# A fused linear attention and GELU network: four edits to the weight sums, the last loads and the last group of tokens

## The chip, the cores and the metric

The kernel runs on one core of one Trainium2 chip. The metric is the device time of one execution in microseconds (us), as the median of several runs. TensorE multiplies matrices into PSUM, VectorE and ScalarE read PSUM and work on SBUF, GpSimd works on SBUF, and SyncE and ScalarE issue the DMA transfers.

## The reference

Two stages follow each other. The first is linear attention over 8 batches, 8 heads, 576 tokens and a head size of 64; the second is a two-layer network on the 4608 tokens that come out.

```python
phi = lambda x: np.where(x > 0, x, np.exp(x) - 1.0) + 1.0
q_p, k_p = phi(q), phi(k)
kv = np.einsum('bhsd,bhse->bhde', k_p, v)
z = np.sum(k_p, axis=2)
attn = np.einsum('bhsd,bhde->bhse', q_p, kv) / (np.einsum('bhsd,bhd->bhs', q_p, z)[..., None] + 1e-06)
x = attn.transpose(0, 2, 1, 3).reshape(4608, 512)
h = x @ w_in                       # 512 -> 2048
g = 0.5 * h * (1 + tanh(c * (h + 0.044715 * h**3)))
out = g @ w_out                    # 2048 -> 512
```

## The kernel before

**Tiles and groups.** The tokens are worked in nine groups of 512. Groups 0 to 7 hold the first 512 tokens of one batch each (MAIN = 512). The last 64 tokens of each batch (REST = 64), 512 in all, make group 8, which the code calls j == B. In group 8, tile t of 128 tokens holds the rest of batches 2t and 2t + 1, one behind the other: partitions 0 to 63 are of the first batch and 64 to 127 of the second.

**One group.** `iteration(j)` runs steps in an order that is written out by hand, and after each step it runs whatever was registered for that slot with `at(j, slot, ...)`. Each engine takes its instructions in this program order, so a slot is also a place in every engine's queue. A group has 16 h steps: `h_mm` (line 390) multiplies a block of 128 columns of w_in with the transposed x into a PSUM bank of 512 columns, and `gelu` (line 400) writes the result to `g` in SBUF as f16. From group 2 on, the product g @ w_out is not formed directly. `Products` takes g and w_out as 2 x 2 blocks and forms seven block products (line 767) in place of eight, in the manner of Strassen and Winograd. This needs sums of blocks of w_out, formed once by `sum_w_out` (line 739), and sums of blocks of g, formed in each group by `Products.sums` and `last_sum` (line 750). The partial results p, z and w stay in PSUM and are added on VectorE by `plus` (line 820) or copied by ScalarE (lines 789 and 803) into two result tiles o1 and o2, which are stored.

**The attention for the next group** runs in between. For phi, ScalarE forms the exponential (`exp_of`, line 220), VectorE the linear part (`linear_of`, line 228) and the smaller of the two (`least_of`, line 234); `cast_v` (line 239) converts v. The products of k and v (line 250), the numerator and denominator (`nab_quads`, line 328) and the division (line 284) follow. Transposes go through the DMA on SyncE's queue (lines 645, 657 and 680).

**Sums of w_out.** `sum_w_out` is four subtractions of [128, 8, 256] in f16. They are given to GpSimd in halves, so eight instructions. The first three write `w_sum` and stand at slot 10 of group 1; the fourth overwrites a quarter of w_out itself and stands at slot 0 of group 2. The first use is in group 2.

**Rest tokens.** `load_rest(m)` fetches q of the rest of batches 2m and 2m + 1 (line 117, two transfers of 128 KB). m = 0 and 1 are loaded at slot 2 of group 4; m = 2 and 3 at slot 1 of group 6. `plan_rest(m)` puts their linear part at slot 6, their exponential at slot 15 and their minimum with its DMA transpose at slot 18, of group 5 for m = 0 and 1 and of group 6 for m = 2 and 3. The tiles that hold phi of the rest tokens come two at a time, so the second pair takes the place of the first.

**Group 8's end.** There is no next group behind which a store could hide. Step 5 stores o2 whole and step 6 first stores the low half of o1 (`self.store(0, self.o1, lo)`). Step 6 then forms the last product in two halves of 128 tokens, both into halves of one PSUM bank z, adds each half and stores it. `store_rest` (line 825) issues two transfers for a tile, one for each batch, on ScalarE's and SyncE's queues:

```python
for s, eng in enumerate((nc.scalar, nc.sync)):
    r0 = (2 * t + s) * S + MAIN
    eng.dma_start(out=out[r0 : r0 + REST, fs], in_=o_sb[REST * s : REST * (s + 1), fs])
```

PSUM has a pool of six banks for h, p, z, w and the like, and a pair of banks for the attention.

Of the kernel before, what the change touches and what calls it, by code (L numbers as in the profile page):

```python
# [10 lines left out]
FP16 = mybir.dt.float16  # L11
AF = mybir.ActivationFunctionType
ALU = mybir.AluOpType
# [3 lines left out]
def kernel(  # L17
# [16 lines left out]
    nc = tc.nc  # L34

    B, H, S, D = q.shape
    d_model, d_ff = moe_w_in.shape
    P = 128
    HP = P // 2
    C = 4  # L40
    MAIN = P * C
    REST = S - MAIN
# [3 lines left out]
    MM = d_ff // P  # L46
    E = D + 1
    N2 = d_model // 2
# [9 lines left out]
    pg = ctx.enter_context(tc.tile_pool(name="pg", bufs=1))  # L58
# [19 lines left out]
    def bank(name, shape, dt=FP32):  # L78
        return ps_b.tile(shape, dt, name=name, tag="b")
# [150 lines left out]
    def least_of(name, b, hs=None):  # L230
        p, e = phi[name, b], exps[name, b]
        if hs:
            p, e = p[:, :, hs, :], e[:, :, hs, :]
        nc.vector.tensor_tensor(p, p, e, op=ALU.min)  # L234
# [153 lines left out]
    def h_mm(h_ps, xt, m, ts=slice(0, MAIN), blocks=range(KM)):  # L388
        for c in blocks:
            nc.tensor.matmul(  # L390
                h_ps[:, ts],
                lhsT=w_in_sb[:, c, P * m : P * (m + 1)],
                rhs=xt[:, c, ts],
                start=(c == 0),
                stop=(c == KM - 1),
                skip_group_check=True,
            )

    def gelu(g, m, h_ps):
        nc.scalar.activation(  # L400
            g[:, :, m, :], h_ps.rearrange("p (a n) -> p a n", a=2), AF.Gelu_apprx_tanh
        )

    h_begun = {0: {}, 1: {}}

# [104 lines left out]
    def at(j, slot, fn, *args):  # L510


        fill.setdefault((j, slot), []).append((fn, args))
# [124 lines left out]
    def plan_rest(m):  # L638
        j = 5 + m // 2

        def least():
            least_of("qr", m)
            if m == 0:
                qts[B] = pt.tile([P, C, NP, P], BF16, name="qt")
            nc.sync.dma_start_transpose(
                out=qts[B][:, m], in_=phi["qr", m][:, 0].rearrange("p h d -> p (h d)")
            )

        at(j, 6, linear_of, "qr", m)
        at(j, 15, exp_of, "qr", m)  # L650
        at(j, 18, least)

# [63 lines left out]
    def o_mm(o_ps, g, t, ms, half=None):  # L716
        for m in ms:
            if m == ms.start + 2 and half:
                run(*half)
            nc.tensor.matmul(  # L720
                o_ps,
                lhsT=g[:, t // 2, m, P * (t % 2) : P * (t % 2 + 1)],
                rhs=w_out_sb[:, :, m, :],
                start=(m == 0),
                stop=(m == MM - 1),
            )
# [4 lines left out]
    def sum_w_out(ns):  # L731

        b11, b21 = (w_out_sb[:, 0, h] for h in ff)
        b12, b22 = (w_out_sb[:, 1, h] for h in ff)
        t1, t2, t4 = (w_sum[:, n] for n in range(3))
        sums = ((t1, b12, b11), (t2, b22, t1), (t4, b21, t2), (b12, b22, b12))
        for out, i0, i1 in sums[ns]:
            for ms in (slice(0, 4), slice(4, 8)):
                nc.gpsimd.tensor_tensor(out[:, ms], i0[:, ms], i1[:, ms], op=ALU.subtract)  # L739

    ff = (slice(0, MM // 2), slice(MM // 2, MM))

    class Products:
# [18 lines left out]
            self.subtract(self.a[0][0], self.a[0][1], self.s[1])  # L762

        def product(self, ps, lhs, rhs, first, ts=range(2)):
            for t in ts:
                for m in range(MM // 2):
                    nc.tensor.matmul(  # L767
                        ps[:, t, :],
                        lhsT=lhs[:, m, P * t : P * (t + 1)],
                        rhs=rhs[:, m, :],  # L770
                        start=(first and t == 0 and m == 0),
                        stop=(m == MM // 2 - 1),
                        skip_group_check=True,
                    )

        def step(self, n):
            j = self.j
            (a11, a12), (a21, a22) = self.a
            (b11, b21), (t3, b22) = [[w_out_sb[:, d, h] for h in ff] for d in range(2)]
            t1, t2, t4 = (w_sum[:, i] for i in range(3))  # L780
            lo, hi = slice(0, N2), slice(N2, d_model)
            if n < 4:
                ps = bank("o_ps", [P, 2, N2])
            if n == 0:
                self.p = ps
                self.product(ps, a11, b11, True)
                self.o1 = pout.tile([P, 2, d_model], FP32, name="o_sb")
                self.o2 = pout.tile([P, 2, d_model], FP32, name="o_sb")
                nc.scalar.copy(self.o1[:, :, hi], ps)
            elif n == 1:  # L790
                self.z = ps
                self.product(ps, self.s[0], t1, True)
            elif n == 2:
                self.product(ps, self.s[1], t2, True)
                self.plus(self.o1[:, :, hi], ps, self.o1[:, :, hi])
            elif n == 3:
                self.w = ps
                self.product(ps, a21, t3, True)
                self.plus(self.o2[:, :, hi], ps, self.o1[:, :, hi])
                self.plus(self.o2[:, :, hi], self.z, self.o2[:, :, hi])  # L800
            elif n == 4:
                self.product(self.p, a12, b21, False)
                nc.scalar.copy(self.o1[:, :, lo], self.p)  # L803
            elif n == 5:
                self.product(self.w, a22, t4, False)
                self.plus(self.o2[:, :, lo], self.w, self.o1[:, :, hi])
                self.store(1, self.o2)
            elif j < B:
                self.product(self.z, a11, b22, False)
                self.plus(self.o1[:, :, hi], self.z, self.o1[:, :, hi])  # L810
                at(j + 1, 0, self.store, 0, self.o1)
            else:
                self.store(0, self.o1, lo)
                for t in range(2):
                    self.product(self.z, a11, b22, False, (t,))
                    self.plus(self.o1[:, t, hi], self.z[:, t], self.o1[:, t, hi])
                    self.store_rest(t, self.o1[:, t], hi)

        def plus(self, out, i0, i1):
            nc.vector.tensor_tensor(out, i0, i1, op=ALU.add)  # L820

        def store_rest(self, t, o_sb, fs):
            for s, eng in enumerate((nc.scalar, nc.sync)):
                r0 = (2 * t + s) * S + MAIN
                eng.dma_start(
                    out=out[r0 : r0 + REST, fs], in_=o_sb[REST * s : REST * (s + 1), fs]
                )

        def store(self, h, o_sb, fs=slice(0, d_model)):

# [7 lines left out]

    def iteration(j):
        xt = xts[j]  # L840
        g = pg.tile([P, 2, MM, MAIN // 2], FP16, name="g")
        hs = [("h", m) for m in range(MM)]
        us = [range(m, m + 4) for m in range(0, MM, 4)]
        if j == 0:
            us[2:3] = range(8, 10), range(10, 12)
            steps = hs + [("o", t, u) for u in us for t in range(C)]
        elif j == 1:
            os = [[("o", t, u) for u in us[i : i + 2] for t in range(C)] for i in (0, 2)]
            steps = hs[:8] + os[0] + hs[8:] + os[1]
        else:  # L850
            products = Products(j, g)
            steps = [hs[i + n] for i in range(MM // 2) for n in (0, MM // 2)]
            steps += [("product", n) for n in range(7)]
            at(j, 7, products.sums, slice(0, 4))
            at(j, 15, products.sums, slice(4, 8))
            at(j, 16, products.last_sum)
        o_pss = {}
        for slot, step in enumerate(steps):
            if step[0] == "h":
                m = step[1]  # L860
                h_ps = h_begun.get(j, {}).get(m)
                if h_ps is None:
                    h_ps = bank("h_ps", [P, MAIN])
                    h_mm(h_ps, xt, m)
                gelu(g, m, h_ps)
            elif step[0] == "product":
                products.step(step[1])
            else:
                t, u = step[1:]
                if u.start == 0:  # L870
                    o_pss[t] = bank("o_ps", [P, d_model])
                o_mm(o_pss[t], g, t, u, half=(j, slot - 0.5))
                if u.stop == MM:
                    finish(j, t, o_pss[t])
            run(j, slot)
# [15 lines left out]
        at(b - 3, 1, load_all_pairs, "v", v, b)  # L891
    for m in range(2):
        at(4, 2, load_rest, m)
        at(6, 1, load_rest, m + 2)
    for j in range(2, 7):
        at(j, 16, gelu_table)
    at(1, 10, sum_w_out, slice(0, 3))
    at(2, 0, sum_w_out, slice(3, 4))

    for j in range(B + 1):  # L900
        iteration(j)
# [30 lines left out]
```

## Time and profile before

| what | value |
|---|---|
| time, median of 3 runs | 277.02 us (276.88 to 278.88) |
| span of the profiled execution | 274.5 us |
| TensorE busy, share of the span | 265.8 us, 97% |
| VectorE / ScalarE / GpSimd busy | 158.3 / 164.1 / 37.1 us |
| granted TensorE clock | 0.998 |
| HBM read and written | 36.70 and 9.44 MB, 168 GB/s over the span |

The span is what the profiler recorded of one execution. An engine's busy share is an average over all stages. In a line of the timeline the first number is the start in us from the span's start, the second the duration in us, then the engine, the line of the kernel, the operation, output<-input, the tile's form and the count; in brackets stands how long the engine had idled before, and which instruction ended that. Engines with a q behind them (SPq, ACTq) are the queues that issue DMA transfers.

### The profile page before, as it was taken

How to read it: one execution, taken by the hardware profiler on the slowest of the kernel's cores; microseconds unless marked ns; L12 is line 12 of the kernel's file. 1: busy time of each engine (PE TensorE's matmuls, PEld its weight loads, DVE VectorE, ACT ScalarE, POOL GpSimd, SP SyncE). 2: the span in 40 equal slices, each digit the busy share in tenths (PEclk: the TensorE clock that was granted, in tenths of full speed). 3: DMA queues.
4: the chain of work that ended last, by engine and by line, in shares of the span. 5: the costliest groups of instructions: out<-in, count | busy, mean ns of one | idle time of the engine just before them, and what ended most of it. 6: DMA issues, size and time to landing. Idle time of an engine off the chain costs nothing.

```text
span 274.5 us, 5840 instructions
## 1 busy us (share of the span) xinstructions
PE 265.8 (97%) x2485; PEld 165.9 (60%) x2485; DVE 158.3 (58%) x246; ACT 164.1 (60%) x224; POOL 37.1 (14%) x29
## 2 busy tenths in 40 slices
PE   8999999999999999999999999999989999999992
PEld 3584456444444686568656865686458646864781
DVE  3850286965669966788648874672376246422431
ACT  4768878794888683578357835763664365036400
POOL 3147309994000000000000000000000000000000
PEclk9999999999999999999999999999999999999999
DMA  7999999985999986993798650328521403030004
GB/s 245 401 406 398 409 405 403 401 326 154 162 331 276 397 123 187 331 264 73 185 389 222 84 189 2 79 47 153 146 57 41 171 2 76 2 153 0 2 0 153
DMA packets 59592, 53.84 MB, mean 196 GB/s; under 512 B 35760, under 2 KB 45488, under 8 KB 59568
## 3 DMA queue, kind: packets, MB, share of 16 engines
q1 hardware_dynamic: 56784, 44.58, 55.3%
q10 hardware_dynamic: 2784, 8.91, 9.0%
q8 instruction: 19, 0.31, 0.5%
q14 instruction: 5, 0.04, 0.0%
HBM read 36.70 MB, written 9.44 MB: 168 GB/s over the span
## 4 chain that ended last, share of the span: by engine, by line
PE 91%; DVE 3%; ACT 2%; DMA 1%; SPq 1%; issue 0%; DVEq 0%
PE h_ps L390 43%; PE o_ps L767 31%; PE o_ps L720 8%; PE w_ps L424 4%; DMA qr<-in_q_dram 1%; PE n_ps L328 1%; PE kv_ps L250 1%; PE n_ps L250 1%; DVE k_p L234 1%; PE n_ps L266 1%; ACT k_e L220 1%; PE t_ps L383 1%; ACT q_e L220 1%; SPq L117 1%; DVE s L750 0%; ACT L220 0%
## 5 line engine op out<-in xcount | busy, mean ns | idle before, releaser
L390 PE MATMUL h_ps<-xt,w_in_sb 128*128 128x512 bf16 (+1 forms) x628 | 128.9, 361 | 0.9 <-DVE xs L284 0.9
L400 ACT ACTIVATE g<-h_ps 128x512 f16<-128x512 f32 x144 | 84.6, 599 | 66.1 <-PE h_ps L390 65.4
L390 PEld LDWEIGHTS <-w_in_sb 128*128 128x128 bf16 x628 | 57.9, 98 | 63.4 <-DVE xs L284 1.3
L767 PEld LDWEIGHTS <-g 128*128 128x128 f16 x560 | 54.8, 98 | 8.5 <-issue 0.7
L767 PE MATMUL o_ps<-w_out_sb,g 128*128 128x256 f16 x448 | 52.5, 273 | 0.5 <-DVE o_sb L820 0.5
L820 DVE TENSOR_TENSOR o_sb<-o_ps,o_sb 128x512 f32<-128x512 f32 (+1 forms) x36 | 24.4, 677 | 30.2 <-PE o_ps L767 28.1
L750 DVE TENSOR_TENSOR s<-g 128x1024 f16<-128x1024 f16 x14 | 9.7, 690 | 36.5 <-ACT g L400 36.5
L720 PE MATMUL o_ps<-w_out_sb,g 128*128 128x512 f16 x128 | 29.4, 379 | 0.0
L284 DVE TENSOR_TENSOR xs<-n_ps,r 128x384 bf16<-128x384 f32 (+2 forms) x43 | 25.4, 592 | 1.5
L767 PE MATMUL o_ps<-w_sum,s 128*128 128x256 f16 x224 | 25.6, 273 | 0.0
L767 PEld LDWEIGHTS <-s 128*128 128x128 f16 x224 | 21.9, 98 | 2.5
L720 PEld LDWEIGHTS <-g 128*128 128x128 f16 x128 | 12.1, 98 | 13.3
L228 DVE TENSOR_SCALAR q_p<-q_x 128x2048 bf16<-128x2048 f32 (+1 forms) x9 | 10.5, 1171 | 13.1 <-DMA q_x<-in_q_dram 13.1
L220 ACT ACTIVATE k_e<-k_x 128x2304 bf16<-128x2304 f32 (+1 forms) x9 | 17.2, 1908 | 0.8 <-DMA k_x<-in_k_dram 0.8
L803 ACT COPY o_sb<-o_ps 128x512 f32<-128x512 f32 x7 | 4.1, 586 | 22.2 <-PE o_ps L767 22.2
L220 ACT ACTIVATE q_e<-q_x 128x2048 bf16<-128x2048 f32 (+1 forms) x9 | 15.5, 1719 | 2.8 <-DMA q_x<-in_q_dram 2.7
L228 DVE TENSOR_SCALAR k_p<-k_x 128x2304 bf16<-128x2304 f32 (+1 forms) x9 | 12.9, 1432 | 4.1 <-DMA k_x<-in_k_dram 4.1
L767 PE MATMUL o_ps<-w_sum,g 128*128 128x256 f16 x112 | 13.4, 273 | 0.0
L239 DVE CAST vp<-v_x 128x2304 bf16<-128x2304 f32 (+1 forms) x9 | 12.9, 1439 | 0.5 <-DMA v_x<-in_v_dram 0.4
L234 DVE TENSOR_TENSOR k_p<-k_p,k_e 128x2304 bf16<-128x2304 bf16 (+1 forms) x9 | 12.0, 1337 | 1.3 <-ACT k_e L220 1.0
L415 ACT ACT_TABLE_LOAD x9 | 11.5, 1283 | 0.2
L739 POOL TENSOR_TENSOR w_sum<-w_out_sb,w_sum 128x1024 f16<-128x1024 f16 x4 | 11.6, 2924 | 0.0
(61 smaller groups left out, 169.7 us busy)
## 6 DMA issues: line engine op xcount, KB each, us to landing
out_dram<-o_sb ACTq DMA_DIRECT2D x16, 512.0 KB, 4.9
k_x<-in_k_dram SPq DMA_DIRECT2D x7, 1152.0 KB, 7.0
v_x<-in_v_dram SPq DMA_DIRECT2D x7, 1152.0 KB, 12.2
q_x<-in_q_dram SPq DMA_DIRECT2D x6, 1024.0 KB, 12.5
w_st<-in_moe_w_in_dram SPq DMA_DIRECT2D x3, 1024.0 KB, 13.5
q_x<-in_q_dram SPq DMA_DIRECT2D x4, 512.0 KB, 8.6
w_st<-in_moe_w_out_dram SPq DMA_DIRECT2D x2, 1024.0 KB, 12.5
w_st<-in_moe_w_out_dram SPq DMA_DIRECT2D x4, 512.0 KB, 11.2
```

The lines of the kernel that those rows point to most:

```text
L220: nc.scalar.activation(o, i, AF.Exp)
L228: nc.vector.tensor_scalar(o, i, 1.0, 1.0, op0=ALU.add, op1=ALU.max)
L234: nc.vector.tensor_tensor(p, p, e, op=ALU.min)
L239: fn(out=vp_paired(b)[:, :, us, 0:D].rearrange("p j u d -> p u j d"), in_=ld["v", b][:, us].rearrange("p u (j d) -> p u j d", d=D),)
L284: nc.vector.tensor_tensor(x_v, n_v[heads + (slice(0, D),)], r[heads + (None,)].to_broadcast(shape + [D]), op=ALU.mult,)
L390: nc.tensor.matmul(h_ps[:, ts], lhsT=w_in_sb[:, c, P * m : P * (m + 1)], rhs=xt[:, c, ts], start=(c == 0), stop=(c == KM - 1), skip_group_ ...
L400: nc.scalar.activation(g[:, :, m, :], h_ps.rearrange("p (a n) -> p a n", a=2), AF.Gelu_apprx_tanh)
L415: nc.scalar.preload_act_table_set("gelu_apprx_tanh_and_others")
L720: nc.tensor.matmul(o_ps, lhsT=g[:, t // 2, m, P * (t % 2) : P * (t % 2 + 1)], rhs=w_out_sb[:, :, m, :], start=(m == 0), stop=(m == MM - 1),)
L739: nc.gpsimd.tensor_tensor(out[:, ms], i0[:, ms], i1[:, ms], op=ALU.subtract)
L767: nc.tensor.matmul(ps[:, t, :], lhsT=lhs[:, m, P * t : P * (t + 1)], rhs=rhs[:, m, :], start=(first and t == 0 and m == 0), stop=(m == MM ...
L820: nc.vector.tensor_tensor(out, i0, i1, op=ALU.add)
```

## The change

Four edits are made together.

1. The four sums of w_out go from GpSimd to VectorE, whole and not in halves. The first three move from slot 10 of group 1 to slot 4, behind the cast of v. The fourth keeps its slot.
2. The second load of rest tokens moves from slot 1 of group 6 to slot 1 of group 5. Their linear part moves from slot 6 of group 6 to slot 0.
3. In group 8 the tokens of the two batches of a tile take turns: partition 2n + s holds token n of batch s. This order comes about when the GELU writes g, with a step of two elements, and g is laid out block by block so that the write can be expressed. A whole tile can then be stored with one transfer of 128 rows; the tiles alternate between the two queues. The low half of o1 is stored right after it is copied, in step 4.
4. In group 8 the sum z lies in two PSUM banks, one for each half of 128 tokens, so that the two halves of the last product do not share a bank.

```diff
+    def gelu(j, g, m, h_ps):
+        g_v, h_v = g[:, :, m, :], h_ps.rearrange("p (a n) -> p a n", a=2)
+        if j == B:
+            g_v = g[:, :, m, :].rearrange("p a (t n s) -> p (a t) s n", t=2, s=2)
+            h_v = h_ps.rearrange("p (t s n) -> p t s n", t=C, s=2)
+        nc.scalar.activation(g_v, h_v, AF.Gelu_apprx_tanh)
...
-        at(j, 6, linear_of, "qr", m)
+        at(j, 6 if j == 5 else 0, linear_of, "qr", m)
...
-            for ms in (slice(0, 4), slice(4, 8)):
-                nc.gpsimd.tensor_tensor(out[:, ms], i0[:, ms], i1[:, ms], op=ALU.subtract)
+            nc.vector.tensor_tensor(out, i0, i1, op=ALU.subtract)
...
-                        ps[:, t, :],
+                        ps[t] if type(ps) is list else ps[:, t, :],
...
-                        start=(first and t == 0 and m == 0),
+                        start=(first and m == 0 and (t == 0 or type(ps) is list)),
...
+            if n == 1 and j == B:
+                ps = [bank("o_ps", [P, N2]) for _ in range(2)]
...
-                self.plus(self.o2[:, :, hi], self.z, self.o2[:, :, hi])
+                if j < B:
+                    self.plus(self.o2[:, :, hi], self.z, self.o2[:, :, hi])
+                else:
+                    for t in range(2):
+                        self.plus(self.o2[:, t, hi], self.z[t], self.o2[:, t, hi])
...
                 nc.scalar.copy(self.o1[:, :, lo], self.p)
+                if j == B:
+                    self.store(0, self.o1, lo)
...
-                self.store(0, self.o1, lo)
                 for t in range(2):
                     self.product(self.z, a11, b22, False, (t,))
-                    self.plus(self.o1[:, t, hi], self.z[:, t], self.o1[:, t, hi])
+                    self.plus(self.o1[:, t, hi], self.z[t], self.o1[:, t, hi])
...
-            for s, eng in enumerate((nc.scalar, nc.sync)):
-                r0 = (2 * t + s) * S + MAIN
-                eng.dma_start(
-                    out=out[r0 : r0 + REST, fs], in_=o_sb[REST * s : REST * (s + 1), fs]
-                )
+            ov = out.rearrange("(t s n) f -> t n s f", s=2, n=S)[t, MAIN:S, :, fs]
+            (nc.scalar, nc.sync)[t % 2].dma_start(
+                out=ov, in_=o_sb[:, fs]
+            )
...
+        if j < B:
+            g = pg.tile([P, 2, MM, MAIN // 2], FP16, name="g")
+        else:
+            g = pg.tile([P, MM, 2, MAIN // 2], FP16, name="g").rearrange("p m a n -> p a m n")
...
-        at(6, 1, load_rest, m + 2)
+        at(5, 1, load_rest, m + 2)
...
-    at(1, 10, sum_w_out, slice(0, 3))
+    at(1, 4, sum_w_out, slice(0, 3))
```

More of the change, by code (lines that the diff above doesn't have):

```diff
@@ L397, in h_mm @@
             )
-    def gelu(g, m, h_ps):
-        nc.scalar.activation(
-            g[:, :, m, :], h_ps.rearrange("p (a n) -> p a n", a=2), AF.Gelu_apprx_tanh
-        )
+    def gelu(j, g, m, h_ps):
[4 more added lines that the diff above has]
+        nc.scalar.activation(g_v, h_v, AF.Gelu_apprx_tanh)
     h_begun = {0: {}, 1: {}}
@@ L781, in step @@
             lo, hi = slice(0, N2), slice(N2, d_model)
-            if n < 4:
+            if n == 1 and j == B:
+                ps = [bank("o_ps", [P, N2]) for _ in range(2)]
+            elif n < 4:
                 ps = bank("o_ps", [P, 2, N2])
@@ L822, in store_rest @@
         def store_rest(self, t, o_sb, fs):
-            for s, eng in enumerate((nc.scalar, nc.sync)):
-                r0 = (2 * t + s) * S + MAIN
-                eng.dma_start(
-                    out=out[r0 : r0 + REST, fs], in_=o_sb[REST * s : REST * (s + 1), fs]
-                )
+            ov = out.rearrange("(t s n) f -> t n s f", s=2, n=S)[t, MAIN:S, :, fs]
+            (nc.scalar, nc.sync)[t % 2].dma_start(
+                out=ov, in_=o_sb[:, fs]
+            )
         def store(self, h, o_sb, fs=slice(0, d_model)):
@@ L840, in iteration @@
         xt = xts[j]
-        g = pg.tile([P, 2, MM, MAIN // 2], FP16, name="g")
+        if j < B:
+            g = pg.tile([P, 2, MM, MAIN // 2], FP16, name="g")
+        else:
+            g = pg.tile([P, MM, 2, MAIN // 2], FP16, name="g").rearrange("p m a n -> p a m n")
         hs = [("h", m) for m in range(MM)]
@@ L864, in iteration @@
                     h_mm(h_ps, xt, m)
-                gelu(g, m, h_ps)
+                gelu(j, g, m, h_ps)
             elif step[0] == "product":
```

## The prediction

> **What bounds the kernel now.** First the page's busy times and slices: TensorE is busy 97% of the span and at 9 in nearly every slice, with the clock at full. So only three things can move the end: TensorE's own work, the few places where it waits, and what lies ahead of its first and behind its last matmul.
>
> ```profile
> PE 265.8 (97%) x2485; PEld 165.9 (60%) x2485; DVE 158.3 (58%) x246; ACT 164.1 (60%) x224; POOL 37.1 (14%) x29
> ...
> PE   8999999999999999999999999999989999999992
> ...
> PEclk9999999999999999999999999999999999999999
> ```
>
> The dip to 8 in slice 29 and the 2 in the last slice are the visible holes. The list of waits for TensorE alone says who made them (total us, times, longest):
>
> ```profile
> PE h_ps L390 <- DVE xs L284: 0.9, 1, 0.9
> PE kv_ps L250 <- DVE k_p L234: 0.6, 1, 0.6
> PE o_ps L767 <- DVE o_sb L820: 0.5, 1, 0.5
> ```
>
> The change touches all three (the other three waits on that list, 1.8 us, lie in the first 15 us, which it does not touch). Then I read the timeline around each. The 0.6 us wait, in group 1:
>
> ```profile
> 48.22 1.83 DVE L228 TENSOR_SCALAR q_p<-q_x 128x2048 bf16<-128x2048 f32 x1
> ...
> 49.98 3.27 DVE L228 TENSOR_SCALAR k_p<-k_x 128x2304 bf16<-128x2304 f32 x1
> ...
> 53.17 3.28 DVE L239 CAST vp<-v_x 128x2304 bf16<-128x2304 f32 x1
> ...
> 58.40 6.40 POOL L739 TENSOR_TENSOR w_out_sb<-w_out_sb 128x1024 f16<-128x1024 f16 x2
> ...
> 60.40 2.41 DVE L234 TENSOR_TENSOR k_p<-k_p,k_e 128x2304 bf16<-128x2304 bf16 x1 [0.79 <-ACT k_e L220]
> ...
> 62.86 0.78 PE L250 MATMUL kv_ps<-vp,k_p 64*64 64x65 bf16 x72 [0.60 <-DVE k_p L234]
> ...
> 72.47 1.35 DVE L228 TENSOR_SCALAR k_p<-k_x 128x2304 bf16<-128x2304 f32 x1
> ...
> 74.87 1.35 DVE L234 TENSOR_TENSOR k_p<-k_p,k_e 128x2304 bf16<-128x2304 bf16 x1
> ```
>
> GpSimd's eight sums run from 42.69 to 64.80. While they run, VectorE takes 3.27 us for a form that takes 1.35 us at 72.47, and 2.41 us for the minimum that takes 1.35 us at 74.87; TensorE waits 0.60 us for that minimum. The 0.9 us wait, in group 6:
>
> ```profile
> 191.19 2.64 SPq L117 DMA_DIRECT2D qr<-in_q_dram  x4
> ...
> 196.16 0.43 DVE L228 TENSOR_SCALAR qr_p<-qr 128x512 bf16<-128x512 f32 x1 [7.20 <-DMA qr<-in_q_dram]
> ...
> 197.39 0.68 DVE L750 TENSOR_TENSOR s<-g 128x1024 f16<-128x1024 f16 x1
> ...
> 200.16 3.63 PE L390 MATMUL h_ps<-xt,w_in_sb 128*128 128x512 bf16 x16 [0.85 <-DVE xs L284]
> ```
>
> The second half of the rest tokens is loaded in the group that uses it; VectorE, in order, stands 7.2 us at its head, the sums of g and the division xs come late, and TensorE waits for the PSUM banks that the division empties. And the tail, with TensorE's end near 269.6 and the span's at 274.5:
>
> ```profile
> 268.05 0.42 DVE L820 TENSOR_TENSOR o_sb<-o_ps,o_sb 128x256 f32<-128x256 f32 x1 [0.18 <-PE o_ps L767]
> 268.53 1.03 PE L767 MATMUL o_ps<-w_out_sb,g 128*128 128x256 f16 x8 [0.52 <-DVE o_sb L820]
> ...
> 269.60 0.42 DVE L820 TENSOR_TENSOR o_sb<-o_ps,o_sb 128x256 f32<-128x256 f32 x1 [1.12 <-PE o_ps L767]
> ...
> 271.54 0.47 ACTq L825 DMA_DIRECT2D out_dram<-o_sb  x1
> ```
>
> The last add ends at 270.02, but the last of 12 stores is issued only at 271.54: each of the two queues works through six stores that began at 267.90, at 0.47 to 0.81 us each.
>
> **What the Trainium skill says.** "SBUF — State Buffer", Who interferes with whom: VectorE and GpSimd share a pair of ports as an exclusive lock; a VectorE operation in a 2-port mode, or with two SBUF inputs beside a GpSimd operation that reads SBUF, blocks or is blocked. The trace agrees: 3.27 against 1.35 us. "VectorE: DVE Perf Modes", the perf-mode tier table: a 16-bit tensor_tensor of 2048 takes 1224 ns; the trace's 128x2048 f16 sum (L750) takes 1.23 us. "SBUF — State Buffer", Door 1 (its note on cachelines): lines of 16 bytes, a step within which is free, up to 8 bf16 elements; the new GELU writes step by two f16. No row of before has such a write. "DMA: Bandwidth & Descriptors", Why a DMA increments its semaphore by 16 and not by 1: the number of DMA engines is the largest up to 16 that divides the outer dimensions on both sides; the new store has 64 and 128 there, so 16. No store of before has that pattern.
>
> **The change part by part.**
>
> 1. *Sums of w_out to VectorE.* Removes 8 GpSimd instructions (22.2 us on an engine nobody waits for). Adds four VectorE tensor_tensor of 128x2048 f16, at 1.23 us by the L750 row: three in group 1 behind the cast of v, one in group 2. What is queued behind the three is the minimum of q, which waits for ScalarE's exponential until 58.35 in any case. Without the lock the three operations ahead cost 1.22 + 1.35 + 1.36 (the uncontended rows of the same forms at 73.74, 72.47 and 78.54) instead of 8.4, so the cast ends near 52.2, or by 54.6 if v lands so late that the cast starts no sooner than before (53.17). Plus 3.7 us: the sums end between 55.9 and 58.3, before 58.35 at both ends. So they are hidden, by ScalarE's exponentials. The minimum of k then runs 60.40 to 61.75 and the kv products can start when TensorE is there, at about 62.26. Gain 0.60 us. The fourth sum falls into 79.9 to 82.8, where VectorE idles 2.93 us for the kv product: nothing.
>
> 2. *Rest loads a group sooner, their linear map at the head of group 6.* The four loads move to about 163 us, when group 5 begins and the transposes of x are not wanted before 171.83. The map then finds its data there; what it waits for is its tile, which the transposes of the first half still read (issued 186.42 to 191.1, about 4 us to land). That is over by about 192 to 195, and the next VectorE work, the sums of g, cannot start before the eighth GELU ends at 195.8. TensorE loses its 0.85 us wait. A second way: by the chain, group 6 takes 188.24 to 216.01 = 27.77 us, group 7 the same TensorE work in 216.01 to 242.85 = 26.84; 0.93. I take 0.90.
>
> 3. *Last product in two banks.* The second half need not wait for the add of the first: 268.53 becomes 268.03. Gain 0.50. The z sum becomes two adds of 0.42 for one of 0.69 at 264 us, where VectorE then idles 2.08: nothing. One more bank is held, five of six; the GELUs have by then emptied all others: nothing.
>
> 4. *One store to a tile; the low half leaves earlier.* 12 stores become 6, three a queue; the two low halves are issued near 266.05, behind the ScalarE copy, instead of behind the others. So at the last add each queue is empty, and the last store goes 0.03 us behind it (as 267.90 follows the add ending 267.87). Gain 271.54 − 270.02 − 0.03 = 1.49. Against it: the last store has 128 KB instead of 64. The DMA rows give 2.6 to 3.0 us to landing for 128 KB and 2.3 to 2.5 for 64: +0.1 to +0.7, but with many in flight; with few I take +0.2.
>
> 5. *Batches in turn.* The GELU of the last group writes steps of two, the sums of g read runs of 256. No row shows the step. Lower bound nothing; upper bound twice the time per element. Exponentials of 512 and 2048 take 0.61 and 1.91 us, so 0.85 ns an element, 0.43 of the GELU's 0.60; doubled it is 1.03 against TensorE's 0.86 a step: 16 × 0.17 = 2.7 us late, with 0.23 us of slack before the second product (the first sum ends 258.02, TensorE comes at 258.25). I take nothing, since the cacheline note allows the step.
>
> Sum: 0.60 + 0.90 + 0.50 + 1.49 − 0.2 = 3.3 us; 277.0 − 3.3 = **273.7 us**, 1.2% less.
>
> **The rivals.**
>
> *The store's end is hidden or handed back.* Not the queue but the landing of the larger stores sets the end, or the larger issue takes longer. For: nearly 3 us lie between the last issue and the span's end. Against: the last issue is 1.5 us behind its data. Gain 2.0 alone: 275.0.
>
> *Strided GELU at twice the time per element.* The 2.5 us of wait eat most: about 276.2. For: no row shows it. Against: item 5.
>
> *Slower: the new store pattern spreads badly.* If the inner pair of batches were taken as the outer dimension, two DMA engines would carry the 1 MB of the last six stores. At 405 GB/s over 16 engines (the page's best slices) one carries 25; 1 MB over two takes 20 us from 266: the end near 288, time about 291. Against: 64 is the outer count.
>
> *More than the sum.* Fewer stores in flight land sooner than 2.5 us, and the head of group 1 moves too: 0.5 to 1 us more, about 272.9.
>
> **How the numbers follow.** Forecast 0.70, store's end handed back 0.12, better 0.10, strided GELU 0.05, slower 0.03. The bound of 1% is 274.25; the forecast has it with some 0.6 us to spare, so I give nine tenths of it and the better case to faster: 0.73. The remainder, the rival at 275.0 and the strided GELU make 0.23; slower 0.04. The range runs from just below the better case, 272.7, to just above the rival, 275.1.
>
> **What would show it.** No GpSimd tensor_tensor, k's map at about 1.35 us and no wait of kv products for k_p; no 7.2 us wait of VectorE for qr, and the chain free of qr; GELUs of the last group still 0.60; no wait between the two halves of the last product; the last issue within 0.1 us of the last add, at some 268.0. Wrong if the last group's GELUs exceed 0.86, if the map at the head of group 6 waits past 196, or if the last store takes over 3.5 us to end.

## The result, and the profile after

The changed kernel takes 273.26 us (273.18 to 273.55) against 276.95 us for the kernel before: the ratio is 0.985, 95% interval 0.981 to 0.990. Run again later, beside other runs of the kernel before, it took 273.67 against 276.56 us, ratio 0.990 (0.988 to 0.992). So 2.9 to 3.7 us are gained; 3.3 had been forecast. The profiled execution has a span of 271.4 us against 274.5.

The page of the changed kernel, its busy times and TensorE's slices:

```profile
PE 263.4 (97%) x2465; PEld 165.8 (61%) x2485; DVE 157.6 (58%) x251; ACT 166.4 (61%) x224; POOL 15.0 (6%) x21
...
PE   8899999999999999999999999999999999999993
```

GpSimd has lost 22 us. VectorE has taken on the four sums and is yet no busier, because its operations beside GpSimd became shorter. ScalarE has gained 2.3 us, where the forecast had put nothing. The dip in slice 29 is gone. TensorE's waits:

```profile
PE w_ps L427 <- DVE warm L182: 1.2, 1, 1.2
PE kv_ps L250 <- DVE vp L239: 0.9, 2, 0.5
PE n_ps L364 <- ACT kvbd L262: 0.4, 1, 0.4
PE t_ps L383 <- DVE xs L373: 0.2, 1, 0.2
```

The three waits shown of before are no longer there; what remains lies in the first 15 us. The timeline of group 1, answering to the 3.27, 3.28 and 2.41 us and the wait of 0.60 us of before:

```profile
49.34 1.35 DVE L228 TENSOR_SCALAR k_p<-k_x 128x2304 bf16<-128x2304 f32 x1
...
50.64 1.36 DVE L239 CAST vp<-v_x 128x2304 bf16<-128x2304 f32 x1
...
51.92 1.22 DVE L741 TENSOR_TENSOR w_sum<-w_out_sb 128x2048 f16<-128x2048 f16 x1
...
53.27 2.48 DVE L741 TENSOR_TENSOR w_sum<-w_out_sb,w_sum 128x2048 f16<-128x2048 f16 x2
...
60.38 1.36 DVE L234 TENSOR_TENSOR k_p<-k_p,k_e 128x2304 bf16<-128x2304 bf16 x1 [0.79 <-ACT k_e L220]
...
62.19 0.78 PE L250 MATMUL kv_ps<-vp,k_p 64*64 64x65 bf16 x72
```

The three sums end at 55.75, well before the exponential at 58.35, and the kv products start at 62.19 instead of 62.86. In group 6 VectorE waits 3.62 us for the transposes instead of 7.2 for the load, and is in time for the sums of g:

```profile
191.92 0.79 DVE L228 TENSOR_SCALAR qr_p<-qr 128x512 bf16<-128x512 f32 x2 [3.62 <-DMA qt<-qr_p]
...
195.14 0.69 DVE L752 TENSOR_TENSOR s<-g 128x1024 f16<-128x1024 f16 x1 [2.43 <-ACT g L405]
...
196.73 5.35 PE L390 MATMUL h_ps<-xt,w_in_sb 128*128 128x512 bf16 x23
```

And the tail: no wait of TensorE between the halves of the last product, and the last store directly behind the last add.

```profile
266.35 0.42 DVE L830 TENSOR_TENSOR o_sb<-o_ps,o_sb 128x256 f32<-128x256 f32 x1 [0.18 <-PE o_ps L770]
267.23 0.43 DVE L830 TENSOR_TENSOR o_sb<-o_ps,o_sb 128x256 f32<-128x256 f32 x1 [0.45 <-PE o_ps L770]
...
267.68 0.54 SPq L834 DMA_DIRECT2D out_dram<-o_sb  x1
```

From that last issue to the end of the span it now takes 3.72 us; before it was 2.92. Something was given back there. Dividing the span between the two profiles by landmarks (the start of the kv products in group 1, of the product in groups 6 and 8, the end of the last add, the last issue, the end):

| step of the prediction | foreseen | between the profiles |
|---|---|---|
| 1, sums of w_out | 0.60 | 0.67 |
| 2, rest loads | 0.90 | 1.03 |
| 3, two banks | 0.50 | 0.68 |
| 4, last issue behind the last add | 1.49 | 1.48 |
| 4, landing of the larger store | −0.2 | −0.80 |
| 5, step in the GELU | 0 | 0 in time; 0.15 us a GELU |
| sum | 3.3 | 3.06 |

### The profile page after: what moved, and what is told of

It reads as the page before. It is cut to its first block, busy times and chain, and to the rows that moved or that the text cites. A ratio compares the mean times of both kernels' runs of the same rounds, so it can differ in the third digit from the quotient of the medians.

```text
span 271.4 us, 5804 instructions
## 1 busy us (share of the span) xinstructions
PE 263.4 (97%) x2465; PEld 165.8 (61%) x2485; DVE 157.6 (58%) x251; ACT 166.4 (61%) x224; POOL 15.0 (6%) x21
## 4 chain that ended last, share of the span: by engine, by line
PE 93%; DMA 3%; SPq 1%; DVE 1%; issue 1%; ACT 0%
PE h_ps L390 46%; PE o_ps L770 32%; PE o_ps L723 10%; DMA v_x<-in_v_dram 3%; PE n_ps L328 1%; PE n_ps L250 1%; PE kv_ps L250 1%; PE n_ps L266 1%; PE t_ps L383 1%; SPq L94 1%; SPq L99 0%; PE t_ps L541 0%; DVE vp L239 0%; DVE xs L373 0%; DVE o_sb L830 0%
## 5 line engine op out<-in xcount | busy, mean ns | idle before, releaser
L405 ACT ACTIVATE g<-h_ps 128x512 f16<-128x512 f32 x144 | 87.0, 616 | 62.2 <-PE h_ps L390 59.8
L228 DVE TENSOR_SCALAR q_p<-q_x 128x2048 bf16<-128x2048 f32 (+1 forms) x9 | 9.9, 1102 | 13.1 <-DMA q_x<-in_q_dram 13.1
L228 DVE TENSOR_SCALAR k_p<-k_x 128x2304 bf16<-128x2304 f32 (+1 forms) x9 | 11.0, 1219 | 4.1 <-DMA k_x<-in_k_dram 4.1
L234 DVE TENSOR_TENSOR q_p<-q_p,q_e 128x2048 bf16<-128x2048 bf16 (+1 forms) x9 | 9.9, 1102 | 3.1 <-ACT q_e L220 3.0
L234 DVE TENSOR_TENSOR k_p<-k_p,k_e 128x2304 bf16<-128x2304 bf16 (+1 forms) x9 | 11.0, 1222 | 1.3 <-ACT k_e L220 0.9
L283 DVE RECIPROCAL r<-n_ps 128x6 f32<-128x6 f32 (+2 forms) x43 | 8.2, 190 | 5.5 <-PE n_ps L266 5.5
```

The lines of the kernel that those rows point to most:

```text
L228: nc.vector.tensor_scalar(o, i, 1.0, 1.0, op0=ALU.add, op1=ALU.max)
L283: nc.vector.reciprocal(r, n_v[heads + (D,)])
L405: nc.scalar.activation(g_v, h_v, AF.Gelu_apprx_tanh)
```

## The experiments

All start from the changed kernel. In the first set the kernel before took 276.25 us, in the second 276.51, in the third 276.56. The changed kernel itself stands in the third set alone, where it took 273.67 us, 0.4 us more than at first. Differences in time of that size, from one set to another, decide nothing, so what follows leans on the traces and on kernels of one set. For the end of the kernel I also use the tail of a profile: its span less the start of group 8's product in the chain. It is 17.80 us before and 16.44 after.

**The sums given back to GpSimd.**

```diff
-            nc.vector.tensor_tensor(out, i0, i1, op=ALU.subtract)
+            for ms in (slice(0, 4), slice(4, 8)):
+                nc.gpsimd.tensor_tensor(out[:, ms], i0[:, ms], i1[:, ms], op=ALU.subtract)
...
-    at(1, 4, sum_w_out, slice(0, 3))
+    at(1, 10, sum_w_out, slice(0, 3))
```

> The changed kernel with the four sums of w_out given back to GpSimd, in halves and in their old slots. Theory (the shared port lock): VectorE's minimum of k in group 1 is again near 2.4 us instead of 1.36, TensorE waits about 0.6 us for it, and the time is 0.6 to 0.7 us above the changed kernel's, about 273.9. Rival (something else gave the 0.67 us, such as the slot or the loads): the minimum stays near 1.4 us or TensorE does not wait, and the time stays within 0.2 of 273.3.

Measured: 273.77 us, ratio 0.991 (0.990 to 0.993), span 272.0. TensorE waits for k_p again and the kv products start at 63.00:

```profile
58.47 2.12 POOL L742 TENSOR_TENSOR w_out_sb<-w_out_sb 128x1024 f16<-128x1024 f16 x1
58.52 3.15 DVE L234 TENSOR_TENSOR q_p<-q_p,q_e 128x2048 bf16<-128x2048 bf16 x1 [2.00 <-ACT q_e L220]
61.60 1.34 DVE L234 TENSOR_TENSOR k_p<-k_p,k_e 128x2304 bf16<-128x2304 bf16 x1
...
63.00 0.78 PE L250 MATMUL kv_ps<-vp,k_p 64*64 64x65 bf16 x72 [0.59 <-DVE k_p L234]
```

So the wait belongs to this edit; the trace shows it, while the time alone would not, as its interval overlaps that of the changed kernel (0.988 to 0.992). But the minimum of k took 1.34 us here, against the expectation: the minimum of q ahead of it took 3.15 and pushed it back to 61.60. The lock struck one operation earlier than the theory said, with the same effect.

**The fourth sum alone on GpSimd.**

```diff
+            if ns.start < 3:
+                nc.vector.tensor_tensor(out, i0, i1, op=ALU.subtract)
+                continue
+            for ms in (slice(0, 4), slice(4, 8)):
+                nc.gpsimd.tensor_tensor(out[:, ms], i0[:, ms], i1[:, ms], op=ALU.subtract)
-            nc.vector.tensor_tensor(out, i0, i1, op=ALU.subtract)
```

> The changed kernel with only the fourth sum, the one that overwrites a quarter of w_out, on GpSimd in two halves; the first three stay on VectorE. Theory: the lock hurts where a GpSimd sum lies beside the minimum of k at 60.4 us, and that is the fourth sum alone; the k map and the cast of v stay at 1.35 us, but the minimum is again slow, TensorE waits about 0.6 us, about 273.9. Rival: the first three sums, which slowed the map and the cast, made the loss by delaying VectorE's queue; then this kernel has no wait and stays near 273.3.

Measured: 274.05 us, ratio 0.993 (0.991 to 0.995), span 272.3. Its timeline in group 1:

```profile
58.15 2.13 POOL L745 TENSOR_TENSOR w_out_sb<-w_out_sb 128x1024 f16<-128x1024 f16 x1 [15.50 <-PE o_ps L723]
...
58.43 2.92 DVE L234 TENSOR_TENSOR q_p<-q_p,q_e 128x2048 bf16<-128x2048 bf16 x1 [2.65 <-ACT q_e L220]
...
61.27 1.35 DVE L234 TENSOR_TENSOR k_p<-k_p,k_e 128x2304 bf16<-128x2304 bf16 x1
...
62.68 0.78 PE L250 MATMUL kv_ps<-vp,k_p 64*64 64x65 bf16 x72 [0.36 <-DVE k_p L234]
```

One GpSimd instruction of 2.13 us, begun 0.3 us before the minimum of q, lengthens that from 1.23 to 2.92, and TensorE waits 0.36 us. With all eight it was 0.59, since the instructions of the first three sums held this one back to 58.47. Those three slowed much more VectorE work, but work that was waiting for ScalarE anyhow. So the rival falls: of eight GpSimd instructions, those of the fourth sum set the wait. Of the 0.89 us by which the span is longer than the changed kernel's, 0.49 show at the kv products; the others come from a tail of 16.83 us, whose code is that of the changed kernel.

**The rest loads given back to group 6.**

```diff
-        at(j, 6 if j == 5 else 0, linear_of, "qr", m)
+        at(j, 6, linear_of, "qr", m)
...
-        at(5, 1, load_rest, m + 2)
+        at(6, 1, load_rest, m + 2)
```

> The changed kernel with the second load of rest tokens back in group 6 and their map back at slot 6. Theory: VectorE waits about 7 us for qr again, TensorE about 0.9 us for the division, group 6 is 0.9 to 1.0 us longer, about 274.3. Rival: part of the 1.03 us by which group 6 became shorter came from elsewhere, such as VectorE's lighter queue; then less than 0.5 us comes back, below 273.8.

Measured: 274.0 us, ratio 0.993 (0.991 to 0.995), span 272.2.

```profile
188.55 3.39 SPq L117 DMA_DIRECT2D qr<-in_q_dram  x4
...
194.84 0.43 DVE L228 TENSOR_SCALAR qr_p<-qr 128x512 bf16<-128x512 f32 x1 [6.57 <-DMA qr<-in_q_dram]
...
198.87 3.63 PE L390 MATMUL h_ps<-xt,w_in_sb 128*128 128x512 bf16 x16 [0.26 <-DVE xs L284]
```

The wait returns, but TensorE loses 0.26 us, and from the product of group 5 to that of group 6 it is 27.18 us against 26.74 in the changed kernel and 27.77 before. By these 0.44 us the rival is right; the time, 274.0, is on the side of the theory, but 0.37 us of the longer span lie in a tail of 16.81 us, whose code is unchanged. So the edit is worth 0.4 to 1.0 us. The loads were issued at 188.55 here and at 191.19 before, since the two transposes ahead of them on SyncE's queue took 2.72 us and not 4.68. The same two transposes in the profiles of the kernel before, of the changed kernel when it was run again, and of the kernel with the sums undone:

```profile
186.42 4.68 SPq L645 DMA_TRANSPOSE qt<-qr_p  x2
...
186.79 4.08 SPq L648 DMA_TRANSPOSE qt<-qr_p  x2
...
186.56 2.70 SPq L648 DMA_TRANSPOSE qt<-qr_p  x2
```

In the first profile of the changed kernel they took 2.71 us. So they differ from execution to execution with the same code, and it was not VectorE's lighter queue in group 1 that made them short. Part of the 1.03 us between the profiles is therefore likely chance.

**The sum z in one bank again.**

```diff
-            if n == 1 and j == B:
-                ps = [bank("o_ps", [P, N2]) for _ in range(2)]
-            elif n < 4:
+            if n < 4:
...
-                        ps[t] if type(ps) is list else ps[:, t, :],
+                        ps[:, t, :],
```

> The changed kernel with the sum z of group 8 in one PSUM bank again. Theory: the second half of the last product waits for the first half's add, 0.5 us, and nothing behind it can make that up: the last add and with it the end come 0.5 to 0.7 us later, about 273.9. Rival: the end is set by the stores ahead of the last one, whose landing hides the wait; then the end moves by less than 0.2 us.

Measured: 273.37 us, ratio 0.990 (0.989 to 0.992), span 271.6: the rival. The wait is back in full, and the last add ends 0.80 us later, 0.12 of which come from earlier groups:

```profile
266.48 0.42 DVE L828 TENSOR_TENSOR o_sb<-o_ps,o_sb 128x256 f32<-128x256 f32 x1 [0.18 <-PE o_ps L770]
266.95 1.03 PE L770 MATMUL o_ps<-w_out_sb,g 128*128 128x256 f16 x8 [0.52 <-DVE o_sb L828]
...
268.02 0.42 DVE L828 TENSOR_TENSOR o_sb<-o_ps,o_sb 128x256 f32<-128x256 f32 x1 [1.12 <-PE o_ps L770]
```

But the tail is 16.51 against 16.44 us. In the changed kernel the last store lands 2.70 us after its issue, 0.32 behind the one before it; here it lands after 2.10 us, 0.31 behind the one before it. The stores ahead hide the wait. The windows of the changed kernel's tail show with what (last columns: the DMA engines' busy share, GB/s):

```profile
core 0: us, PE busy (x) PEld busy (x) DVE busy (x) ACT busy (x) POOL busy (x), PEclk, DMA share, GB/s
...
266.50:267.50 1.00, 0.69 (x7) 0.37 (x4) 0.55 (x2) 0.00 (x0) 0.00 (x0) 1.00 0.08 27
267.50:268.50 1.00, 0.00 (x0) 0.00 (x0) 0.15 (x1) 0.00 (x0) 0.00 (x0) 1.00 1.04 401
268.50:269.50 1.00, 0.00 (x0) 0.00 (x0) 0.00 (x0) 0.00 (x0) 0.00 (x0) 1.00 0.99 354
```

Four stores of 768 KB in all are issued between 266.20 and 267.68. The DMA engines are full with them for two microseconds, at 401 and 354 GB/s, and the last bytes go when they have passed.

**Two stores to a tile, the low half early.**

```diff
-            g_v = g[:, :, m, :].rearrange("p a (t n s) -> p (a t) s n", t=2, s=2)
-            h_v = h_ps.rearrange("p (t s n) -> p t s n", t=C, s=2)
+            pass
...
-            (nc.scalar, nc.sync)[t % 2].dma_start(
-                out=ov, in_=o_sb[:, fs]
-            )
+            for s, eng in enumerate((nc.scalar, nc.sync)):
+                r0 = (2 * t + s) * S + MAIN
+                eng.dma_start(
+                    out=out[r0 : r0 + REST, fs], in_=o_sb[REST * s : REST * (s + 1), fs]
+                )
```

> The changed kernel with the old order of tokens in group 8 (no step in the GELU, g laid out as before) and two stores of 64 rows to a tile, twelve in all, but with the low half still stored right after its copy. Theory A (the queue's backlog was the cost, and the early low half alone takes most of it away): at the last add each queue has one store of the first half ahead, the last issue is 0.1 to 0.6 us behind the add, the smaller last stores end about 3.0 us after issue instead of 3.7, and the time is within 0.3 of the changed kernel's 273.3. Theory B (one store to a tile is what gains): twelve stores again pile up, the last issue is over 1 us behind the add, and the time is 1 us or more longer.

Measured: 273.88 us, ratio 0.991 (0.989 to 0.992), tail 17.16. The last issue is at 268.73, 0.83 us behind the last add, between the two theories, and lands after 2.64 us. So one store to a tile is worth some 0.7 us in the tail, and 0.6 us in time against a kernel of the same set that has the changed kernel's tail (the step of one below, 273.30 us). That this comes from the number of issues alone is not shown: with stores of 64 rows the DMA engines moved 244 to 282 GB/s from 267.5 to 270.5, with those of 128 rows in the changed kernel 401 and 354.

**One store to a tile, the low half late.**

```diff
             elif n == 4:
-                if j == B:
-                    self.store(0, self.o1, lo)
...
             else:
+                self.store(0, self.o1, lo)
```

> The changed kernel with one store to a tile, but the low half stored only in step 6, behind the store of the other result tile, as before. Theory A (early low half): three stores a queue begin near 266.2 and take 0.57 us each, so the last is issued near 267.9 to 268.0, 0.2 to 0.3 us later than now, and the landings bunch: 0.3 to 0.6 us longer. Theory B (number of stores alone): the same as the changed kernel within 0.2 us.

Measured: 274.06 us, ratio 0.991 (0.990 to 0.993), tail 17.53. The last issue, at 268.00, is just where theory A put it, but that is not what costs: the stores take 3.4 to 4.0 us from issue to landing, against 2.2 to 3.5 in the changed kernel. All 1 MB goes out in one burst. The low half early is worth some 1.1 us by the tails, but this profile is the slowest of five executions; by the times, 274.06 against 273.30 us for the same kernel with a step of one, it is 0.8 us. Either is more than A allowed.

**The GELU's step.** Two kernels that differ in how the GELU of group 8 writes; both leave the rest tokens in another order than the reference's.

```diff
-            g_v = g[:, :, m, :].rearrange("p a (t n s) -> p (a t) s n", t=2, s=2)
-            h_v = h_ps.rearrange("p (t s n) -> p t s n", t=C, s=2)
+            g_v = g[:, :, m, :].rearrange("p a (t n s) -> p (a t) s n", t=2, s=4)
+            h_v = h_ps.rearrange("p (t s n) -> p t s n", t=C, s=4)
```

> The changed kernel with the GELU of group 8 writing in steps of four f16 (8 bytes) instead of two, so the rest tokens are stored in another order than the reference's. The GELU of group 8 took 0.75 us with a step of two and 0.60 without. Theory A (the cost grows with the step, as fewer elements share a line): 0.9 us or more, over TensorE's 0.86 us a step, so the sums of g come late and the time grows by some 0.3 to 2 us. Theory B (a fixed price for any step): 0.75 again and no change of time. Theory C (a price for each run, as the pattern has more and shorter runs): 8 runs more double the 0.15, so about 0.9 as in A; the next run tells them apart.

```diff
-            g_v = g[:, :, m, :].rearrange("p a (t n s) -> p (a t) s n", t=2, s=2)
+            g_v = g[:, :, m, :].rearrange("p a (t s n) -> p (a t) s n", t=2, s=2)
```

> The changed kernel with its layout of g and its stores, but with the GELU of group 8 writing without a step, so the rest tokens are stored in another order than the reference's. If the step costs: GELU back at 0.60 us; the time is the same within 0.1 us if the 0.15 us are hidden behind TensorE's 0.86 us a step, and up to 0.2 us shorter if the last GELU and the first sum of g behind it are on the path to the second product.

The windows over the 16 GELUs of group 8, with a step of one, two (the changed kernel) and four; the number before (x16) is their busy time:

```profile
241.00:255.80 14.80, 9.55 (x16) 1.00 0.17 71
```

```profile
241.00:255.80 14.80, 11.91 (x16) 1.00 0.17 71
```

```profile
242.00:260.60 18.60, 18.40 (x16) 0.93 0.08 34
```

That is 0.60, 0.74 and 1.15 us a GELU. With a step of one the time is 273.30 us and the tail 16.44, that of the changed kernel: the 0.15 us lie under TensorE's 0.86 a step. With four it is 279.56 us (ratio 1.011, 1.009 to 1.013): the GELUs fall behind, and the loss is far above the 0.3 to 2 us that I gave. About 4.5 us of it lie ahead of the second product, which starts at 259.41 in the chain and not at 254.96: 16 GELUs, each some 0.29 us over TensorE's step. Beside most of the remainder stands the granted clock (the number behind the busy times) in this profile, from the last GELUs on:

```profile
256.00:259.40 3.40, 0.28 (x1) 0.10 (x1) 0.00 (x0) 3.40 (x4) 0.00 (x0) 0.77 0.00 0
259.40:264.00 4.60, 4.59 (x22) 3.28 (x23) 3.21 (x4) 1.68 (x2) 0.00 (x0) 0.50 0.01 4
264.00:269.00 5.00, 5.00 (x45) 4.33 (x44) 1.30 (x2) 0.00 (x0) 0.00 (x0) 0.93 0.00 0
```

TensorE waited for the GELUs and then did the start of the product at half clock; the tail is 18.8 us and not 16.44. Neither my expectation nor the prediction's rival of the strided GELU counted this. Of the theories, B falls, since the price is not fixed. A holds in direction. A plain price for each run, C, would have doubled 0.15 us and not made it 0.55; but step and run length changed together, so which of them costs is not separated.

**The high half earlier still.** The third set asks what the burst costs, and whether less of it makes the two banks pay.

```diff
                         self.plus(self.o2[:, t, hi], self.z[t], self.o2[:, t, hi])
+                    self.store(1, self.o2, hi)
...
-                self.store(1, self.o2)
+                self.store(1, self.o2, slice(0, d_model) if j < B else lo)
```

> The changed kernel itself once more, as the measure for the next three on one chip: 273.3 us, ratio to before 0.985 to 0.990.

> The changed kernel with the high half of the second result tile stored as soon as it is added, in step 3 (near 263.5 us), so that only its low half remains for step 5. In the changed kernel the last four stores, 768 KB, are issued between 266.2 and 267.7, and land one behind the other, 0.3 us for 128 KB, the last at 270.4. Theory (the tail is bound by these bytes, not by the last add): 256 KB fewer in the burst, so the last store lands 2.1 to 2.3 us after its issue instead of 2.7, and the time is 0.3 to 0.6 us less. Rival (the last store's own latency binds): no change within 0.15 us.

> The kernel with the early high half, with the sum z of group 8 back in one PSUM bank. In the changed kernel two banks brought the last add 0.67 us forward, but the end only about 0.1. Theory (the burst of stores hid it): without the burst the wait shows in the end, 0.4 to 0.7 us longer than the kernel with the early high half. Rival (two banks gain nothing for another reason): the same within 0.15 us.

> The kernel with the early high half, with the very last store cut into two of 64 rows, one on each queue. The smallest last stores seen so far (64 KB, in the kernel before) landed 1.92 us after their issue, against 2.1 at best for 128 KB. If the last store's own size is now what binds: 0.1 to 0.3 us less than the kernel with the early high half. If ScalarE's queue is still busy with the first half's store: no gain.

| kernel | time, us | ratio to before | tail, us |
|---|---|---|---|
| changed, once more | 273.67 | 0.990 (0.988 to 0.992) | 16.45 |
| high half early | 273.10 | 0.988 (0.986 to 0.990) | 16.15 |
| the same, z in one bank | 273.23 | 0.988 (0.986 to 0.990) | 16.33 |
| high half early, last store in two | 273.00 | 0.987 (0.986 to 0.989) | 16.11 |

The direction is the theory's, 0.3 us in the tail, but the intervals overlap, and the banks gain 0.18 us in the tail and not 0.4 to 0.7. The windows of the kernel with the high half early, the first of them from its earlier stores:

```profile
267.00:267.50 0.50, 0.50 (x7) 0.46 (x5) 0.33 (x1) 0.00 (x0) 0.00 (x0) 1.00 1.09 381
...
267.50:268.50 1.00, 0.85 (x8) 0.51 (x6) 0.54 (x2) 0.00 (x0) 0.00 (x0) 1.00 0.08 25
268.50:269.50 1.00, 0.00 (x0) 0.00 (x0) 0.31 (x1) 0.00 (x0) 0.00 (x0) 1.00 0.78 258
269.50:270.50 1.00, 0.00 (x0) 0.00 (x0) 0.00 (x0) 0.00 (x0) 0.00 (x0) 1.00 0.76 264
```

A third fewer bytes, but they run at 260 GB/s, and the burst is two microseconds as before. The stores are now all of rows of 1 KB, but the rows are not what slows them: just before, stores of the same rows moved 381 GB/s. In the burst the DMA engines are busy for three quarters of the time, and its four stores are issued over 1.48 us, from 267.36 to 268.84; so what stretches it now is most likely the pace of issue, which was not varied by itself. The kernel with the last store in two has the lowest time of all, but its interval reaches into that of the changed kernel.

Two bounds on such readings. With the same tail code, the profiles with the sums and the rest loads undone have tails of 16.26 and 16.81 us (last landing after 2.23 and 3.07 us), so in a single profile 0.3 us decides little, and the 0.07 and 0.18 us of the banks only say that the gain is small. In the second of the two the burst moved 410 and 358 GB/s, no less than in the changed kernel, and 9 GB/s in the microsecond behind it: the last landing waits for a few late packets. And two profiles of the third set, the changed kernel among them, hold a wait that the first had not:

```profile
PE n_ps L328 <- DMA qt<-q_p: 0.6, 1, 0.6
```

In group 2 TensorE now arrives 0.67 us earlier for q, whose DMA transposes do not always land earlier (up to 9.3 us there, 7.0 in the first profile). Part of step 1's gain is lost in such executions.

## Why the prediction was right, point by point

**The bound.** TensorE at 97% with a few named waits was the right reading: removing the waits moved the later work by a little more than the waits, 0.67 us from group 1 on and 1.70 from group 6 on, without a new one in the first profile.

**Step 1** held: the sums are hidden, their end at 55.75 is 0.15 ahead of my 55.9 to 58.3, and the lock is what costs. The Trainium skill, "SBUF — State Buffer", Who interferes with whom, speaks of a loser that fully blocks; the traces agree. When the minimum of q began, the GpSimd instruction beside it had 1.85 us left with the fourth sum alone, and 2.07 us with all four; the minimum took 1.69 and 1.92 us more than its 1.23. That the minimum of k is the operation struck, as the experiments expected, was too narrow.

**Step 2** held in mechanism; its size, 1.03 between the profiles but 0.44 when undone, depends on transposes ahead in the queue, whose time I had not seen to vary. My 4 us to their landing was the median of four; the two that matter took 5.9 and 7.0 us in the profile of before.

**Step 3** was mis-sized. The last add came 0.68 us earlier, more than the 0.50, because the 16 matmuls in one stretch take 1.91 us where two stretches of eight took 1.04 and 1.03. But in the end the two banks are worth 0.07 us in the tail, 0.18 with the high half early. I had counted the wait as on the path that sets the end; the burst of stores was on that path beside it.

**Step 4**: the last issue, 1.48 for 1.49, is right to the hundredth, and its price is the term that failed: I took +0.2 for the larger store, with few in flight. It was 0.80, because they are not few: 640 KB, issued up to 1.5 us earlier, stand ahead of it, and the engines move 350 to 400 GB/s. Where the store before had landed 0.9 us sooner (high half early, z in one bank), 128 KB took 2.04 us to land against 1.92 for 64 KB, so the 0.2 was right for an empty queue. It is the first rival in a mild form. Against this the early low half, which I had only as a way to an empty queue, takes a quarter of all bytes out of the burst and is worth 0.8 to 1.1 us by itself. So steps 3 and 4 together gave 1.36 us where I had 1.79.

**Step 5** had the right effect for a reason that does not hold. The skill's note on cachelines ("SBUF — State Buffer", Door 1) let me take a step of two as free. It costs 0.15 us a GELU, a step of four 0.55; the measurement decides. My upper bound for twice the time, 1.03 us, was near what four costs. Only TensorE's slower pace hid it, which was luck.

**The signs and the sum.** One of the three signs of being wrong came true: the last store takes 3.72 us to the end, over the 3.5. The GELUs of group 8, expected at 0.60 us, took 0.74, under the 0.86 that would have been the second sign. The rival of a badly spread store is gone, as the burst filled all 16 DMA engines. The sum is close nonetheless, since steps 1 to 3 gave 0.38 us more than foreseen between the profiles, in step 2 likely in part by chance, and step 4 gave 0.61 less.

## What to carry to other kernels

At the end of a kernel count bytes as well as issues: what is stored in the last three microseconds leaves at the DMA engines' rate, and bringing the last add forward gained almost nothing here while earlier stores still filled them. Send out whatever is finished early, in transfers as large as the data allow: one of 128 rows did better here than two of 64. And before an operation goes to GpSimd, ask which VectorE operation lies beside it, and who waits for that one: much of the delay is free, one instruction of it was not.

## What was not expected of the hardware

ScalarE's time for 512 f16 results depended on how they were laid down: 0.60 us in one run, 0.74 in steps of two, 1.15 in steps of four. Stores of 128 KB from 128 rows landed 0.3 us behind each other when they queued, and 2.04 us after issue when the one before had landed 0.9 us sooner. Stores of 128 rows filled the DMA engines with 354 to 401 GB/s, also in rows of 1 KB (381); those of 64 rows moved 244 to 282. And after a stretch of 3.4 us in which TensorE was busy for 0.28, its granted clock read 0.50 over the next 4.6 us.
